# Summing and storing the last 1,024 numbers of a gated attention and FFN step in 16 rows of 64 columns and not in 4 rows of 256

## The chip, the cores and the metric

The kernel runs on one core of a Trainium2 chip. The metric is the device time of one execution in microseconds (us), the median of several runs. The kernel is written by hand for the five engines of a core: TensorE (PE, matmul; PEld is its weight load), VectorE (DVE), ScalarE (ACT), GpSimd (POOL) and SyncE (SP). SP only issues DMAs here. Each engine has an instruction stream of its own, and they meet through semaphores.

## The reference

One token x of 1,024 numbers goes through two branches, and a gate mixes them:

```python
g = sigmoid((x * gate_w).sum())
a = attention(x)      # 32 query heads, 4 key/value heads, cache of 65,536 positions, head size 128, then @ wo
r = sigmoid(x @ w_r)
b = x + r * ((silu(x @ w_gate) * (x @ w_up)) @ w_down)   # F = 3,584
out = g * a + (1 - g) * b                                # 1,024 numbers
```

Everything is float32. Keys, values and weights together are 346 MB and are read once; the output is 4 KB.

## The kernel before, in words

**The stream.** All large inputs are laid out on the host in the order of their use, in tiles of 128 partitions. SP loads the tiles one after the other into three buffers (`stream`, shown as `st`). First come 4 groups of attention, one for each key/value head (L126), then six tiles of 14,336 columns (L128, L132): gate, up and down weights of the FFN. The last two tiles are loaded in pieces, each with a semaphore of its own (`ENDS`, L132), so that PE can begin before the whole tile is there. The last tile holds blocks 14 to 27 of the down weights, and its pieces end behind 6, 10, 12, 13, 13.75 and 14 blocks of 1,024 columns: 3,072, 2,048, 1,024, 512, 384 and 128 KB.

**The attention groups** (the hardware loop from L305) leave the result of the output projection in the PSUM tile `att`. DVE takes it over to `att_sb` in SBUF with gate and residual (L265).

**The FFN.** L382 sums gate and up. ACT and DVE work out the hidden values, and `hp` holds them transposed: 28 blocks of 32 columns, where only the first column of each block is not zero. The down product takes block b of `hp` as the 32 columns of weights and 1,024 columns of the stream as the moving operand. A matmul of 128 x 32 fills one quarter of the array (PSUM partitions 32j to 32j+31), and four of them, j = 0 to 3, run side by side. In the trace a float32 matmul of the program is two MATMULs with a LDWEIGHTS each, so that the counts of the profile are twice those of the code. Blocks 0 to 23 (`EARLY`) are summed into `att` (L392) in 512 columns; DVE adds them to `att_sb` (L277).

**The last four blocks**, 24 to 27, are the part that the change touches (L397 to L414). Here the output is cut in four quarters of 256 columns, and quarter j stands in row 32j. Each quarter is cut again in two pieces, `PIECES`: columns 0 to 191 are summed in the PSUM tile `y`, columns 192 to 255 in the PSUM tile `acc`. At block 26 `att_sb` is added with the selector `halves` as weights (L404), matmul by matmul between those of the stream (L409). For block 27 the host has put the stream's columns in the order of the pieces, so that `y` is complete after the piece of 384 KB and `acc` after the piece of 128 KB. PE runs all this in program order, and `tail()` puts the wait for a piece of the stream ahead of the first matmul that reads it.

**The end.** After the last matmul on `y` (mark "first") ACT copies 128 x 192 from `y` to `fin` in SBUF (L182); after the last matmul on `acc` (mark "last") DVE copies 128 x 64 to the other columns of `fin` (L280). SP waits for ACT (L134) and for DVE (L135), stores rows 0, 32, 64 and 96 of `fin` (L136), waits until the store has landed (L140), clears the semaphores, and the kernel is over.

```python
sp.wait_ge(sems["acted"], ACTED["first"])
sp.wait_ge(sems["d2s"], 1)
sp.dma_start(
    out.rearrange("(j n) -> j n", j=4), fin[::32, :]
).then_inc(sems["done"], 16)
```

At the start of the kernel POOL fills some tiles with zeros, `halves` among them (L147), and DVE writes the selector into column 0 of each of its two halves (L224).

Of the kernel before, what the change touches and what calls it, by code (L numbers as in the profile page):

```python
# [4 lines left out]
AF = mybir.ActivationFunctionType  # L5
# [3 lines left out]
P = 128  # L9
D = 1024  # L10
G = 4
# [3 lines left out]
F = 3584  # L15
CH = 8192
NCH = SK // CH
NM = CH // 512
NB = CH // P
KB = D // P  # L20
NQ = D // 4
FB = F // P
FN = F // 8
SCALE = DH ** -0.5
# [6 lines left out]
TAIL = 14336  # L31
NTAIL = 3 * KB * F // TAIL

ENDS = {NTAIL - 2: [8 * D, TAIL], NTAIL - 1: [6 * D, 10 * D, 12 * D, 13 * D, 13 * D + 768, TAIL]}

PIECES = [(0, 192), (192, NQ)]

EARLY = 24


HEAD = ["q", "qt"] + [f"s{c}" for c in range(NCH)] + ["mx"] + [f"v{c}" for c in range(NCH)] + ["o", "w"]
MARKS = ["dot"] + [f"{m} {g}" for g in range(G) for m in HEAD]
MARKS += ["gate 0", "gate 1", "up 0", "up 1", "early", "first", "last"]
MARK = {m: i + 1 for i, m in enumerate(MARKS)}

LAST = ["s0", "s2", "s4", "s6", "v0", "v2", "v4", "v6", "w"]

ACTS = ["sig"] + [f"{m}{c} {g}" for g in range(G) for m in "se" for c in range(NCH)] + ["hid", "first"]
ACTED = {m: i + 1 for i, m in enumerate(ACTS)}


def gated_mix_kernel(nc, x, vecs, heads, ffn, out):

# [18 lines left out]
    pe, act, dve, pool, sp = nc.tensor, nc.scalar, nc.vector, nc.gpsimd, nc.sync  # L74

    stream = [nc.alloc_sbuf_tensor(f"st{b}", [P, 2 * CH], F32, align_bytes=256)[:, :] for b in range(BUFS)]
    scores = nc.alloc_sbuf_tensor("s", [P, NCH, 512], F32)[:, :, :]
    pts = nc.alloc_sbuf_tensor("pt", [P, 2, 512], F32)[:, :, :]

    hid = scores[:, 0:2, :].rearrange("p a n -> p (a n)")[:, : FB * 32]  # L80
    hp = scores[:, 2:4, :].rearrange("p a n -> p (a n)")[:, : FB * 32]
    att_sb = scores[:, 4, :]
    zeros = scores[:, 5, :]
    fin = scores[:, 7, :NQ]

    o_sb = scores[:, 0, :].rearrange("p (s d) -> p s d", s=4)
    q_sb, lb = scores[:, 1, :], scores[:, 2, :P]
# [1 line left out]
    def sb(name, *shape):  # L89
        t = nc.alloc_sbuf_tensor(name, [P, *shape], F32)  # L90
        return t[tuple(slice(None) for _ in range(len(shape) + 1))]

    xk = sb("xk", 3, KB)
    x_row, ident, ones, md = sb("x_row", 2 * NQ), sb("ident", P), sb("ones", P), sb("md", P)
    sel, sel8, nsel, sel4 = sb("sel", 32), sb("sel8", HG), sb("nsel", HG), sb("sel4", 4)
    half, halves = sb("half", 2), sb("halves", 2, 32)
    xp, qp, op = sb("xp", KB, 32), sb("qp", 4 * (32 + HG)), sb("op", HG, 32)
    dots, dsum, sig, rest = sb("dots", 2, KB), sb("dsum", 2), sb("sig", 2), sb("rest", 2)
    mx, sums, mh, rl = sb("mx", NCH), sb("sums", NCH), sb("mh", HG), sb("rl", HG)
    m1, nb, l1 = sb("m1", 1), sb("nb", 1), sb("l1", 1)  # L100
    gate = sig[:, 0:1]

    def psum(name, *shape):
        return nc.alloc_psum_tensor(name, [P, *shape])[tuple(slice(None) for _ in range(len(shape) + 1))]

    ps_u, ps_f = psum("ps_u", 2, 512), psum("ps_f", 2, 512)
    ps_s = [ps_u[:, i, :] for i in range(2)]
    acc, ps_m, att, y = psum("acc", 512), psum("ps_m", P), psum("att", 512), psum("y", NQ)

    banks = [y, acc]  # L110

    names = ["done", "fed", "x0", "x1", "x2", "acted", "pooled", "marked", "d2p", "d2a", "d2s", "self"]
    names += [f"ld{b}" for b in range(BUFS)] + [f"end{i}" for i in range(sum(map(len, ENDS.values())))]
    sems = {n: nc.alloc_semaphore(n) for n in names}
# [5 lines left out]
    for i in range(G * PER + NTAIL):  # L120
        b = i % BUFS
        if i >= BUFS:
            g, l = divmod(i - BUFS, PER)
            sp.wait_ge(sems["marked"], MARK[f"{LAST[l]} {g}" if g < G else ["gate 0", "gate 1", "up 0"][l]])
        if i < G * PER:
            sp.dma_start(stream[b], heads[i]).then_inc(sems[f"ld{b}"], 16)  # L126
        elif i - G * PER not in ENDS:
            sp.dma_start(stream[b][:, :TAIL], ffn[i - G * PER]).then_inc(sems[f"ld{b}"], 16)  # L128
        else:
            cuts = ENDS[i - G * PER]  # L130
            for c0, c1 in zip([0] + cuts, cuts):
                sp.dma_start(stream[b][:, c0:c1], ffn[i - G * PER, :, c0:c1]).then_inc(sems[f"end{len(ends)}"], 16)  # L132
                ends.append((i, c0, c1))
    sp.wait_ge(sems["acted"], ACTED["first"])  # L134
    sp.wait_ge(sems["d2s"], 1)  # L135
    sp.dma_start(  # L136
        out.rearrange("(j n) -> j n", j=4), fin[::32, :]
    ).then_inc(sems["done"], 16)
    sp.wait_ge(sems["done"], 16)
    sp.sem_clear(range(nums[0], nums[-1] + 1))  # L140

# [4 lines left out]
    for t in (xp, qp, zeros, halves, op):  # L146
# [4 lines left out]
        out=ident, in_=ident, compare_op=ALU.not_equal, fill=1.0, base=0, pattern=[[-1, P]], channel_multiplier=1  # L151
# [3 lines left out]
    acted = []  # L155

    def tell(ins, name):
        acted.append(name)
        return ins.then_inc(sems["acted"])
# [17 lines left out]
            )  # L177
    act.wait_ge(sems["marked"], MARK["gate 1"])
    tell(act.activation(hid.rearrange("p (e n) -> p e n", e=2), ps_f[:, :, :FN], AF.Exp, scale=-1.0), "hid")  # L179
    act.wait_ge(sems["marked"], MARK["first"])  # L180
    c0, c1 = PIECES[0]
    tell(act.activation(fin[:, c0:c1], banks[0][:, : c1 - c0], AF.Copy), "first")  # L182
    assert acted == ACTS


# [35 lines left out]
    then(dve.tensor_copy(sel4, ident.rearrange("p (j h) -> p j h", h=32)[:, :, 0]))  # L221

    then(dve.tensor_add(half, sel4[:, :2], sel4[:, 2:]))
    dve.tensor_copy(halves[:, :, 0], half)  # L224
    then(dve.tensor_reduce(sel8, ident.rearrange("p (a h) -> p h a", h=HG), AX.X, ALU.add))
    then(dve.tensor_scalar_mul(nsel, sel8, -SCALE))
    for g in range(G):
# [10 lines left out]
        for c in range(NCH):  # L238
            acted_on(f"s{c} {g}")
            ins = dve.tensor_reduce(mx[:, c : c + 1], scores[:, c, :], AX.X, ALU.max)  # L240
# [35 lines left out]
    after("early")  # L276
    to_pe(dve.tensor_add(att_sb, att, att_sb))  # L277
    after("last")
    c0, c1 = PIECES[1]
    dve.tensor_copy(fin[:, c0:c1], banks[1][:, : c1 - c0]).then_inc(sems["d2s"])  # L280


    marks = []
# [1 line left out]
    def mark(ins, name):  # L285
        marks.append(name)
        ins.then_inc(sems["marked"])
# [17 lines left out]
    with pe.Fori(0, G):  # L305
        loaded(0)
        for k in range(KB):
            for f in range(2):
                j = 2 * (k % 2) + f
                ins = pe.matmul(  # L310
                    ps_s[0][32 * j : 32 * j + 32, :], xp[:, k, :],
                    unit(0)[:, k * D + f * 512 : k * D + (f + 1) * 512], start=(k < 2), stop=(k >= KB - 2),
                )
        mark(ins, "q")
        take("d2p")
        for e in range(4):
            ins = pe.matmul(ps_m[:, 2 * e : 2 * e + 2], q_sb[:, e * DH : (e + 1) * DH], half, start=True, stop=True)
        mark(ins, "qt")
        take("d2p")
        for c in range(NCH):  # L320
# [3 lines left out]
            for s in range(4):  # L324
                for j in range(4):
                    ins = pe.matmul(  # L326
                        ps_s[c % 2][32 * j : 32 * j + 32, :], qp[:, 32 * s : 32 * s + 32],
                        unit(1 + c)[:, (4 * s + j) * 512 : (4 * s + j + 1) * 512], start=(s == 0), stop=(s == 3),
                    )
# [3 lines left out]
        for c in range(NCH):  # L333
            loaded(1 + NCH + c)
            take("d2p")
            for m in range(NM):
                j = m % 4
                ins = pe.matmul(  # L338
                    acc[32 * j : 32 * j + 32, :], pts[:, c % 2, 32 * m : 32 * m + 32],
                    unit(1 + NCH + c)[:, m * 512 : (m + 1) * 512], start=(c == 0 and m < 4),  # L340
                    stop=(c == NCH - 1 and m >= NM - 4),
                )
# [3 lines left out]
        for s in range(4):  # L346
            ins = pe.matmul(
                ps_m[:, HG : 2 * HG], o_sb[:, s, :], sel[:, HG * s : HG * s + HG], start=(s == 0), stop=(s == 3)
            )
        mark(ins, "o")  # L350
        take("d2p")
        for h in range(HG):
            for f in range(2):
                j = 2 * (h % 2) + f
                ins = pe.matmul(  # L355
                    att[32 * j : 32 * j + 32, :], op[:, h, :],
                    unit(UNITS - 1)[:, h * D + f * 512 : h * D + (f + 1) * 512], start=False, stop=False,
                    skip_group_check=True,
                )
# [4 lines left out]
    def tail(first, n):  # L364
        i, c = divmod(first, TAIL)
        assert c + n <= TAIL
        if i < min(ENDS):
            if c == 0:
                take(f"ld{(G * PER + i) % BUFS}", 16)
        else:  # L370
            for e, (i1, c0, _) in enumerate(ends):
                if (i1 - G * PER, c0) == (i, c):
                    pe.wait_ge(sems[f"end{e}"], 16)
        return stream[(G * PER + i) % BUFS][:, c : c + n]


    for i, part in enumerate(("gate", "up")):
        ps = (ps_f, ps_u)[i]
        for k in range(KB):
            for e in range(2):  # L380
                for j in range(4):
                    ins = pe.matmul(  # L382
                        ps[32 * j : 32 * j + 32, e, :FN], xp[:, k, :], tail((i * KB + k) * F + (2 * j + e) * FN, FN),
                        start=(k == 0), stop=(k == KB - 1),
                    )
# [3 lines left out]
    for b in range(EARLY):  # L389
        for f in range(2):  # L390
            j = 2 * (b % 2) + f
            ins = pe.matmul(  # L392
                att[32 * j : 32 * j + 32, :], hp[:, 32 * b : 32 * b + 32], tail(2 * KB * F + b * D + f * 512, 512),
                start=(b < 2), stop=(b >= EARLY - 2),
            )
    mark(ins, "early")
    for b in range(EARLY, FB):  # L397
        if b == EARLY + 2:
            take("d2p")
        for bank, (c0, c1) in zip(banks, PIECES):  # L400
            n = c1 - c0
            for j in range(4):
                if b == EARLY + 2:
                    pe.matmul(  # L404
                        bank[32 * j : 32 * j + 32, :n], halves[:, j // 2, :],
                        att_sb[:, j % 2 * NQ + c0 : j % 2 * NQ + c1], start=False, stop=False,
                    )
                at = 4 * c0 + j * n if b == FB - 1 else j * NQ + c0
                ins = pe.matmul(  # L409
                    bank[32 * j : 32 * j + 32, :n], hp[:, 32 * b : 32 * b + 32], tail(2 * KB * F + b * D + at, n),  # L410
                    start=(b == EARLY), stop=(b == FB - 1),
                )
            if b == FB - 1:
                mark(ins, "first" if c0 == 0 else "last")  # L414
    assert marks == MARKS


# [29 lines left out]
```

## Time and profile before

| what | value |
|---|---|
| time, median of 3 runs | 805.84 us (805.73 to 806.34) |
| the profiled execution's own time | 805.78 us |
| its span, first to last instruction | 804.5 us |
| read from HBM | 346.05 MB, 430 GB/s over the span |
| PE, PEld, DVE, ACT busy | 51%, 15%, 9%, 6% of the span |
| mean granted TensorE clock | 0.750 |

The profile is of one execution. Its time is 1.3 us more than its span, for what lies around the instructions. The page gives busy shares, the span in 40 slices, the DMA queues, the chain of work that ended last, and the costliest groups of instructions. Views of the trace give single stretches: the timeline has start, duration, engine, line, operation, output<-input, shape and count, and in brackets the idle time before it and what ended it. Matmuls overlap, so a row of eight matmuls lasts from the first start to the last end. The trace's times are counted from the first instruction.

### The profile page before, as it was taken

The page shows a single profiled execution, that of the slowest core. Times are in us where ns is not written, and L with a number is a line of the kernel's source. Part 1 is how long each engine was busy: PE and PEld are TensorE (multiplying, and loading weights), DVE is VectorE, ACT ScalarE, POOL GpSimd, SP SyncE. Part 2 cuts the span into 40 slices and gives each one's busy share as a digit, 9 for nine tenths or more (in the row PEclk, how much of TensorE's full clock was granted, in tenths as well). Part 3 has the DMA queues.
Part 4 walks back from the last instruction along what each step waited for, and adds up shares of the span by engine and source line. Part 5 has one row for each costly group of instructions (what it writes and reads, how often), then busy time and mean ns, then how long its engine had stood idle before and what let it go on. Part 6 is the DMA issues. An engine that isn't in the chain of part 4 may idle for free. (4 is left out here: it accounts for less than half of the span.)

```text
span 804.5 us, 6124 instructions
## 1 busy us (share of the span) xinstructions
PE 407.5 (51%) x2826; PEld 122.0 (15%) x2826; DVE 72.3 (9%) x135; ACT 44.8 (6%) x100; POOL 2.5 (0%) x13
## 2 busy tenths in 40 slices
PE   0544464455654564545544454456444545464466
PEld 0211111111111121111111111112111111121122
DVE  0200010000000020000100110000000100000310
ACT  0000030000000030000000110000000300000000
POOL 1000000000000000000000000000000000000000
PEclk9977767768767677677877586777776866787778
DMA  9999999999999999999999999999999999999998
GB/s 418 417 418 466 415 424 460 417 428 453 420 430 450 424 431 446 427 430 446 427 430 443 430 430 443 430 431 430 440 433 427 443 430 430 429 448 426 439 413 342
DMA packets 7078, 346.20 MB, mean 430 GB/s; under 512 B 918, under 2 KB 1050, under 8 KB 1308
## 3 DMA queue, kind: packets, MB, share of 16 engines
q1 hardware_dynamic: 6920, 346.04, 99.4%
q8 instruction: 8, 0.13, 0.1%
q10 hardware_dynamic: 148, 0.02, 0.0%
q14 instruction: 2, 0.02, 0.0%
HBM read 346.05 MB, written 0.00 MB: 430 GB/s over the span
## 5 line engine op out<-in xcount | busy, mean ns | idle before, releaser
L326 PE MATMUL ps_u<-st,qp 128*32 128x512 f32 x1024 | 152.5, 759 | 149.1 <-PEq L290 149.1
L338 PE MATMUL acc<-st,pt 128*32 128x512 f32 x1024 | 152.3, 757 | 144.1 <-PEq L290 144.1
L338 PEld LDWEIGHTS acc<-st,pt 128*32 128x32 f32 x1024 | 43.5, 135 | 250.0 <-issue 250.0
L326 PEld LDWEIGHTS ps_u<-st,qp 128*32 128x32 f32 x1024 | 41.4, 135 | 256.3 <-issue 256.3
L171 ACT ACTIVATE s<-ps_u 128x512 f32<-128x512 f32 x32 | 19.1, 597 | 560.4 <-PE ps_u L326 560.4
L240 DVE TENSOR_REDUCE mx<-s 128x1 f32<-128x512 f32 x32 | 22.0, 686 | 284.2 <-ACT s L171 284.2
L255 DVE STREAM_TRANSPOSE pt<-s 128x512 f32<-128x512 f32 x32 | 22.7, 711 | 198.0 <-PE acc L338 194.4
L310 PE MATMUL ps_u<-st,xp 128*32 128x512 f32 x128 | 23.3, 893 | 22.1 <-PEq L290 22.1
L382 PE MATMUL ps_u<-st,xp 128*32 128x448 f32 x128 | 17.1, 703 | 16.9 <-PEq L290 16.9
L382 PE MATMUL ps_f<-st,xp 128*32 128x448 f32 x128 | 16.8, 691 | 13.3 <-PEq L290 13.3
L176 ACT ACTIVATE s<-s,nb 128x512 f32<-128x512 f32 x32 | 22.6, 708 | 10.4 <-DVE nb L250 10.4
L392 PE MATMUL att<-st,s 128*32 128x512 f32 x96 | 14.9, 776 | 7.5 <-DMA st<-in_ffn 4.9
L355 PE MATMUL att<-st,op 128*32 128x512 f32 x128 | 14.6, 594 | 2.4 <-PEq L290 2.4
L301 PE MATMUL ps_m<-dsum,ones 128*128 128x2 f32 x2 | 0.6, 350 | 23.5 <-PEq L290 23.5
L310 PEld LDWEIGHTS ps_u<-st,xp 128*32 128x32 f32 x128 | 5.9, 158 | 40.1 <-issue 40.1
L382 PEld LDWEIGHTS ps_u<-st,xp 128*32 128x32 f32 x128 | 5.3, 139 | 28.6 <-issue 28.6
L259 DVE COPY s<-acc 128x512 f32<-128x512 f32 x4 | 2.8, 692 | 71.6 <-PE acc L338 71.6
L382 PEld LDWEIGHTS ps_f<-st,xp 128*32 128x32 f32 x128 | 5.2, 135 | 25.1 <-issue 25.1
L229 DVE COPY s<-ps_u 128x512 f32<-128x512 f32 x4 | 2.8, 692 | 53.5 <-PE ps_u L310 53.5
L179 ACT ACTIVATE s<-ps_f 128x896 f32<-128x896 f32 x1 | 0.9, 917 | 105.4 <-PE ps_f L382 105.4
L392 PEld LDWEIGHTS att<-st,s 128*32 128x32 f32 x96 | 3.7, 134 | 18.6 <-issue 10.7
L332 PE MATMUL ps_m<-md,ones 128*128 128x128 f32 x8 | 1.8, 311 | 8.2 <-PEq L290 8.2
(69 smaller groups left out, 68.9 us busy)
## 6 DMA issues: line engine op xcount, KB each, us to landing
st<-in_ffn SPq DMA_DIRECT2D x4, 7168.0 KB, 43.3
st<-in_ffn SPq DMA_DIRECT2D x2, 3072.0 KB, 37.1
st<-in_ffn SPq DMA_DIRECT2D x1, 4096.0 KB, 34.9
st<-in_ffn SPq DMA_DIRECT2D x1, 2048.0 KB, 36.9
st<-in_ffn SPq DMA_DIRECT2D x1, 1024.0 KB, 38.9
st<-in_heads SPq DMA_DIRECT2D x36, 48.1
st<-in_ffn SPq DMA_DIRECT2D x1, 512.0 KB, 39.7
st<-in_ffn SPq DMA_DIRECT2D x1, 384.0 KB, 40.2
```

Source lines behind the costliest of these rows:

```text
L171: tell(act.activation(scores[:, c, :], ps_s[c % 2], AF.Copy), f"s{c} {g}")
L176: act.activation(t, t, AF.Exp, bias=nb, scale=SCALE, accum_out=sums[:, c : c + 1]), f"e{c} {g}"
L229: to_pe(dve.tensor_copy(q_sb, ps_s[0]))
L240: ins = dve.tensor_reduce(mx[:, c : c + 1], scores[:, c, :], AX.X, ALU.max)
L255: to_pe(dve.transpose(pts[:, c % 2, :], scores[:, c, :]))
L259: to_pe(dve.tensor_copy(o_sb, acc.rearrange("p (s d) -> p s d", s=4)))
L310: ins = pe.matmul(ps_s[0][32 * j : 32 * j + 32, :], xp[:, k, :], unit(0)[:, k * D + f * 512 : k * D + (f + 1) * 512], start=(k < 2), stop= ...
L326: ins = pe.matmul(ps_s[c % 2][32 * j : 32 * j + 32, :], qp[:, 32 * s : 32 * s + 32], unit(1 + c)[:, (4 * s + j) * 512 : (4 * s + j + 1) * ...
L338: ins = pe.matmul(acc[32 * j : 32 * j + 32, :], pts[:, c % 2, 32 * m : 32 * m + 32], unit(1 + NCH + c)[:, m * 512 : (m + 1) * 512], start= ...
L355: ins = pe.matmul(att[32 * j : 32 * j + 32, :], op[:, h, :], unit(UNITS - 1)[:, h * D + f * 512 : h * D + (f + 1) * 512], start=False, sto ...
L382: ins = pe.matmul(ps[32 * j : 32 * j + 32, e, :FN], xp[:, k, :], tail((i * KB + k) * F + (2 * j + e) * FN, FN), start=(k == 0), stop=(k == ...
L392: ins = pe.matmul(att[32 * j : 32 * j + 32, :], hp[:, 32 * b : 32 * b + 32], tail(2 * KB * F + b * D + f * 512, 512), start=(b < 2), stop= ...
```

## The change

The output is cut in 16 rows of 64 columns (`NR`): piece c of quarter j stands in row 32j + 8c. For this the weights are read 8c columns further left (`hp[:, 32b - 8c : ...]`), so that the one column that is not zero stands at column 8c; the columns ahead of it are zeros of the block before. The selector `halves` is 64 columns wide, with its ones in column 32, and is shifted in the same way. All is summed in `y`, which is now 128 x 64; `acc` isn't used here any more, and the mark "first" and ACT's copy are gone. `att_sb` is added ahead of all matmuls of block 26 and not between them. DVE copies `y` in one instruction. SP waits once, and stores 16 rows of 256 bytes (partitions 0, 8, 16, ..., 120). The pieces of the stream are of the same sizes; within block 27 the host orders the columns by c, so that the piece of 384 KB has c = 0 to 2 and the piece of 128 KB has c = 3.

```diff
+NR = NQ // 4
-ENDS = {NTAIL - 2: [8 * D, TAIL], NTAIL - 1: [6 * D, 10 * D, 12 * D, 13 * D, 13 * D + 768, TAIL]}
-PIECES = [(0, 192), (192, NQ)]
+ENDS = {NTAIL - 2: [8 * D, TAIL], NTAIL - 1: [6 * D, 10 * D, 12 * D, 13 * D, 13 * D + 12 * NR, TAIL]}
...
-    fin = scores[:, 7, :NQ]
+    fin = scores[:, 7, :NR]
...
-    half, halves = sb("half", 2), sb("halves", 2, 32)
+    half, halves = sb("half", 2), sb("halves", 2, 64)
...
-    acc, ps_m, att, y = psum("acc", 512), psum("ps_m", P), psum("att", 512), psum("y", NQ)
-    banks = [y, acc]
+    acc, ps_m, att, y = psum("acc", 512), psum("ps_m", P), psum("att", 512), psum("y", NR)
...
-    sp.wait_ge(sems["acted"], ACTED["first"])
     sp.wait_ge(sems["d2s"], 1)
-    sp.dma_start(
-        out.rearrange("(j n) -> j n", j=4), fin[::32, :]
-    ).then_inc(sems["done"], 16)
+    sp.dma_start(out.rearrange("(i n) -> i n", i=16), fin[::8, :]).then_inc(sems["done"], 16)
...
-    act.wait_ge(sems["marked"], MARK["first"])
-    c0, c1 = PIECES[0]
-    tell(act.activation(fin[:, c0:c1], banks[0][:, : c1 - c0], AF.Copy), "first")
...
-    dve.tensor_copy(halves[:, :, 0], half)
+    dve.tensor_copy(halves[:, :, 32], half)
...
     after("last")
-    c0, c1 = PIECES[1]
-    dve.tensor_copy(fin[:, c0:c1], banks[1][:, : c1 - c0]).then_inc(sems["d2s"])
+    dve.tensor_copy(fin, y).then_inc(sems["d2s"])
...
     for b in range(EARLY, FB):
         if b == EARLY + 2:
             take("d2p")
-        for bank, (c0, c1) in zip(banks, PIECES):
-            n = c1 - c0
+            for c in range(4):
+                for j in range(4):
+                    pe.matmul(
+                        y[32 * j : 32 * j + 32, :], halves[:, j // 2, 32 - 8 * c : 64 - 8 * c],
+                        att_sb[:, j % 2 * NQ + c * NR : j % 2 * NQ + (c + 1) * NR], start=False, stop=False,
+                    )
+        for c in range(4):
             for j in range(4):
-                if b == EARLY + 2:
-                    pe.matmul(
-                        bank[32 * j : 32 * j + 32, :n], halves[:, j // 2, :],
-                        att_sb[:, j % 2 * NQ + c0 : j % 2 * NQ + c1], start=False, stop=False,
-                    )
-                at = 4 * c0 + j * n if b == FB - 1 else j * NQ + c0
+                at = 4 * c + j if b == FB - 1 else 4 * j + c
                 ins = pe.matmul(
-                    bank[32 * j : 32 * j + 32, :n], hp[:, 32 * b : 32 * b + 32], tail(2 * KB * F + b * D + at, n),
-                    start=(b == EARLY), stop=(b == FB - 1),
+                    y[32 * j : 32 * j + 32, :], hp[:, 32 * b - 8 * c : 32 * b - 8 * c + 32],
+                    tail(2 * KB * F + b * D + at * NR, NR), start=(b == EARLY and c == 0),
+                    stop=(b == FB - 1 and c == 3),
                 )
-            if b == FB - 1:
-                mark(ins, "first" if c0 == 0 else "last")
+    mark(ins, "last")
...
-    last = down[:, -1].reshape(P, 4, NQ)
-    down[:, -1] = np.concatenate([last[:, :, c0:c1].reshape(P, -1) for c0, c1 in PIECES], axis=1)
+    down[:, -1] = down[:, -1].reshape(P, 4, 4, NR).transpose(0, 2, 1, 3).reshape(P, D)
```

More of the change, by code (lines that the diff above doesn't have):

```diff
@@ L42 @@
 MARKS = ["dot"] + [f"{m} {g}" for g in range(G) for m in HEAD]
-MARKS += ["gate 0", "gate 1", "up 0", "up 1", "early", "first", "last"]
+MARKS += ["gate 0", "gate 1", "up 0", "up 1", "early", "last"]
 MARK = {m: i + 1 for i, m in enumerate(MARKS)}
 LAST = ["s0", "s2", "s4", "s6", "v0", "v2", "v4", "v6", "w"]
-ACTS = ["sig"] + [f"{m}{c} {g}" for g in range(G) for m in "se" for c in range(NCH)] + ["hid", "first"]
+ACTS = ["sig"] + [f"{m}{c} {g}" for g in range(G) for m in "se" for c in range(NCH)] + ["hid"]
 ACTED = {m: i + 1 for i, m in enumerate(ACTS)}
```

## The prediction

> **What bounds the kernel now.** I began with the page's DMA queues and its chain of work that ended last.
>
> ```profile
> q1 hardware_dynamic: 6920, 346.04, 99.4%
> HBM read 346.05 MB, written 0.00 MB: 430 GB/s over the span
> DMA 5%; PE 1%; SPq 0%; DVE 0%; issue 0%
> ```
>
> The 16 DMA engines are busy with the stream for 99.4% of the span, so nearly all of the 804.5 us is the reading of 346 MB, which the change leaves as it is: same bytes, same sizes of pieces. What can move is what lies behind the stream. The chain in order of time shows how it ends:
>
> ```profile
> 759.67 0.33 SPq L132
> 760.00 0.04 issue
> 760.04 0.43 SPq L132
> ...
> 760.52 38.89 DMA st<-in_ffn
> ...
> 799.46 0.53 PE y L409 x8
> ...
> 802.20 0.16 PE acc L409 x8
> 802.36 0.02 issue
> 802.38 0.23 DVE s L280
> ```
>
> From 799.46 on it is PE, then DVE's copy, and behind them stands the store, which this view doesn't reach. So I read the timeline of the last 5 us (start, duration, engine, line, what):
>
> ```profile
> 799.01 0.69 DVE L277 TENSOR_TENSOR s<-att,s 128x512 f32<-128x512 f32 x1 [20.00 <-PE att L392]
> 799.45 0.16 PEld L409 LDWEIGHTS y<-st,s 128*32 128x32 f32 x8 [1.42 <-DMA st<-in_ffn]
> 799.46 0.53 PE L409 MATMUL y<-st,s 128*32 128x192 f32 x8 [0.51 <-DMA st<-in_ffn]
> 799.92 0.51 PE L409 MATMUL y<-st,s 128*32 128x192 f32 x8
> 800.24 0.29 PE L409 MATMUL acc<-st,s 128*32 128x64 f32 x8
> 800.35 0.49 PE L404 MATMUL y<-s,halves 128*32 128x192 f32 x2
> 800.72 0.11 PEld L409 LDWEIGHTS y<-st,s 128*32 128x32 f32 x1 [0.26 <-DMA st<-in_ffn]
> 801.67 0.53 PE L409 MATMUL y<-st,s 128*32 128x192 f32 x8
> 801.96 0.19 PEld L409 LDWEIGHTS acc<-st,s 128*32 128x32 f32 x8
> 802.02 0.29 PE L409 MATMUL acc<-st,s 128*32 128x64 f32 x8
> 802.27 0.33 ACT L182 ACTIVATE s<-y 128x192 f32<-128x192 f32 x1 [58.66 <-PE y L409]
> 802.38 0.23 DVE L280 COPY s<-acc 128x64 f32<-128x64 f32 x1 [2.68 <-PE acc L409]
> 802.70 0.63 SPq L136 DMA_DIRECT2D out<-s  x1
> ```
>
> The reader is to see four stretches. Blocks 24 and 25 run from 799.46 to 800.35. Block 26 with the sum of `att_sb` waits at 800.72 for its piece of the stream, and then PE has work up to 801.67. Block 27 ends with eight matmuls that start from 802.02. Behind them come the copies, 802.27 to 802.61, the store's issue, 802.70 to 803.33, and its landing:
>
> ```profile
> SPq L135 <- DVE s L280: 40.2, 1, 40.2
> SPq L140 <- DMA out<-s: 1.1, 1, 1.1
> ```
>
> SP's last wait but one is for DVE; then it waits 1.1 us for the store, up to about 804.4. Of the 2.4 us behind PE's last starts, 1.7 us are the store.
>
> **The change part by part.**
>
> *PE, the four blocks.* Price 0. A group of eight starts (four j, two passes) lasts 800.35 - 800.24 = 0.11 us at 64 columns and 800.24 - 799.92 = 0.32 us at 192. Three groups of 64 take 0.33 us, so four make a block of 0.44 us in place of 0.43. There are 160 starts in the five rounds (four blocks and `att_sb`) instead of 80, each with a weight load. By these groups it is the columns that cost, not the starts: blocks 24 and 25 end at 800.35 as now.
>
> *The sum of `att_sb` moved ahead of block 26.* Its input is ready at 799.70 (the row of L277), long before. Now two starts of it fit ahead of the wait that ends at 800.72 and the rest come behind; then all 32 can run from 800.35 to 800.79, and block 26 to 801.23. That is 0.4 us earlier than today, and it is worth nothing, since what is late next is the stream: the windows give, per stretch, the length, the busy times, the granted clock, and the DMA engines' share and GB/s.
>
> ```profile
> 792.00:796.00 4.00, 3.83 (x20) 1.00 (x24) 0.00 (x0) 0.00 (x0) 0.00 (x0) 0.50 1.02 436
> 799.40:800.35 0.95, 0.89 (x32) 0.77 (x33) 0.30 (x1) 0.00 (x0) 0.00 (x0) 1.00 0.86 336
> 800.35:801.67 1.32, 1.32 (x44) 0.98 (x36) 0.00 (x0) 0.00 (x0) 0.00 (x0) 1.00 0.46 171
> 801.67:802.38 0.71, 0.65 (x25) 0.35 (x17) 0.00 (x0) 0.11 (x1) 0.00 (x0) 1.00 0.00 0
> ```
>
> Data still come in during the third stretch. The pieces of 512 and 384 KB follow each other: at 430 GB/s the second is 0.9 us behind the first, whose wait ended at 800.72, so it is there at about 801.6, and block 27 can't start much before 801.67. The last 128 KB come 0.3 us later, which fits the weight loads that start at 801.96 (0.29 us behind the block's start, where blocks without a wait have 0.2). In block 27 the three first groups then run from 801.67 to 802.00, and the last eight starts come at 802.00 to 802.02, where they are now. Bounds: 0.05 us earlier to, if the last piece costs a new start, 0.1 later.
>
> *The copies.* Price 0. ACT's copy ends at 802.60 and DVE's at 802.61, so taking ACT's off frees nothing; DVE copies the same 128 x 64 in 0.23 us, from another PSUM tile. Bounds: 0 and 0.02 us.
>
> *SP's waits.* One wait and not two. Between DVE's end (802.61) and the issue (802.70) lie 0.09 us; in the chain an issue with one wait starts about 0.02 us behind what it waited for (759.67). Gain between 0 and 0.07; I take 0.04.
>
> *The store's issue.* The lines of the issues, with minimum, median and maximum in ns:
>
> ```profile
> L126 SPq DMA_DIRECT2D st<-in_heads x36: 327/328/432, 0.7 to 651.4; - x36
> L136 SPq DMA_DIRECT2D out<-s x1: 633/633/633, 802.7 to 802.7; - x1
> L163 ACTq DMA_DIRECT2D x_row<-in_x x1: 1058/1058/1058, 1.3 to 1.3; - x1
> ```
>
> Loads of 128 rows are issued in 0.33 us, the store of 4 rows takes 0.63, the load of 2 rows 1.06. Fewer rows take longer, not more. Sixteen rows lie between 0.33 and 0.63, a gain of 0.30 to 0. I take the whole 0.30, on the inference that what costs is the number of engines left out: 16 rows can be shared out among the 16 DMA engines as 128 can, 2 and 4 can't.
>
> *The store's landing.* Price 0. After the issue 1.1 us pass. Sixteen packets of 256 bytes take the place of four of 1 KB. The DMA view of 802.70 to 804.50 in 40 slices of 0.045 us shows the packets themselves:
>
> ```profile
> GB/s 0 0 0 0 0 0 0 0 0 0 0 0 0 0 0 0 0 0 0 0 0 0 0 0 0 0 0 23 46 23 0 0 0 0 0 0 0 0 0 0
> ```
>
> They move in three slices, 0.135 us from 803.92 on; 0.6 us pass before and 0.35 behind them. Smaller packets can save no more than 0.1. The other way, 16 packets to finish instead of 4 could at most double the time behind them: 0.35 later. The nearest row is this store itself, with the same 4 KB, so I take its 1.1 us unchanged. [...]
>
> *At the start.* Price 0. POOL fills a `halves` of twice the size, and DVE writes its ones into another column.
>
> ```profile
> 2.23 0.15 POOL L147 MEMSET halves<- 128x64 f32 x1
> 22.88 0.17 DVE L205 COPY xp<-xk 128x8 f32<-128x8 f32 x1 [22.88 <-DMA xk<-in_vecs]
> ```
>
> Even 0.15 us more on POOL at 2.2 us is covered by DVE's first instruction, which waits for a load until 22.88; without that cover it would be 0.15.
>
> *Sum.* 0 + 0 + 0 - 0.04 - 0.30 + 0 = -0.34 us, all of it behind PE. The profiled execution took 805.78 (span 804.5 and 1.3 around it): 805.44. The median of the runs is 0.06 above it: 805.5. With the small bounds together (0.05 + 0.02 + 0.07 + 0.30 + 0.1 gained; 0.1 + 0.35 lost) the case spans 805.3 to 806.3; its own range is 805.2 to 805.8.
>
> **The rivals.**
>
> *A, PE can't start 64-column matmuls that fast (slower).* The groups of 64 columns stand between wide ones, during which the next instructions can queue up; 160 narrow starts in a row are nowhere in this trace. What it holds over a long stretch is 32 starts in 0.89 us, 28 ns each. At that pace 160 starts take 4.48 us from 799.46, to 803.94 instead of 802.13: 1.81 later, less the 0.34 gained, 807.3. It makes the kernel slower from 19 ns a start on: (802.13 - 799.46 + 0.34) / 160. Against it stand the two groups of eight in 0.11 us, 14 ns a start. [...]
>
> *B, the store is no cheaper (no gain).* The issue stays at 0.63, which gives 805.8, or the small writes land 0.35 later, which gives 805.85, or both, 806.2. For it: no row with 16 rows, no small write. Against it: the three issue rows.
>
> *C, PE waits for its own instructions.* The code grows by 160 PE instructions.
>
> ```profile
> q8 instruction: 8, 0.13, 0.1%
> ```
>
> Eight fetches of 16 KB took 0.1% of 16 engines' span, between 0.05 and 0.15%, so 0.8 to 2.4 us each. One more of them in the open gives 806.3 to 807.9. Against it: block 27 has no idle time but that for the stream, so instructions are there in advance.
>
> **How the numbers follow.** Forecast 0.65 at 805.5; B 0.17 (805.8 to 806.2); A 0.10 (806.3 to 807.6); C 0.05; 0.03 for anything else, the clock below among it. The three runs lie 0.6 us apart, which I add below: low 805.0. Above, the range takes in B and A's 807.3, leaving out less than 2 in 10 in all. 0.2% is 1.6 us, about what a measurement of this kernel can tell from no change: faster means below 804.2, which no term here reaches (0.03); slower means above 807.45, the upper parts of A and C and what I don't see (0.09); within, 0.88.
>
> **What would show it.** Right: in the changed kernel L136 takes about 0.33 us and the wait of L140 about 1.1; the groups of eight on `y` follow every 0.11 us; block 27 starts at the landing of its piece, and DVE's copy about 0.7 us behind that. Wrong: groups further apart than 0.15 us (A); L136 at 0.6 or L140's wait at 1.4 (B); an idle stretch of PE in blocks 24 to 27 with no DMA behind it (C). The prediction also fails if the stream itself gets faster or slower, or if the last stage runs at the granted clock of 0.50 that the stretch at 792 shows and not at 1.00; then each of the five rounds takes 0.44 us more, in either kernel.

## The result, and the profile after

The changed kernel takes 807.21 us, median of 22 runs (806.72 to 807.71), against 805.84 (805.63 to 806.34) for the kernel before: a ratio of 1.0016, 95% interval 1.0010 to 1.0022. It is 1.4 us slower: 0.16%, and the slowest run of the kernel before (806.34) is still faster than the fastest of the changed one (806.72). The profiled execution took 807.03 us, with a span of 805.7, against 805.78 and 804.5.

The chain of work that ended last, in the changed kernel, in order of time (start, duration, what), its last seven pieces:

```profile
760.95 40.79 DMA st<-in_ffn
801.75 0.04 issue
801.79 0.42 PE y L401 x14
802.22 0.92 issue
803.14 0.51 PE y L401 x18
803.65 0.02 issue
803.67 0.23 DVE s L272
```

In the middle of block 27 stands a piece of 0.92 us called "issue": PE waits for nothing that the profile shows. The timeline of the changed kernel has the same stretch by instruction:

```profile
799.60 0.94 PEld L401 LDWEIGHTS y<-st,s 128*32 128x32 f32 x64 [1.42 <-DMA st<-in_ffn]
799.60 1.10 PE L401 MATMUL y<-st,s 128*32 128x64 f32 x64 [0.51 <-DMA st<-in_ffn]
800.52 0.63 PE L394 MATMUL y<-s,halves 128*32 128x64 f32 x32
800.97 0.63 PE L401 MATMUL y<-st,s 128*32 128x64 f32 x32
801.79 0.42 PE L401 MATMUL y<-st,s 128*32 128x64 f32 x14 [0.20 <-DMA st<-in_ffn]
803.14 0.49 PE L401 MATMUL y<-st,s 128*32 128x64 f32 x18 [0.92 <-issue]
803.14 0.33 PEld L401 LDWEIGHTS y<-st,s 128*32 128x32 f32 x17 [1.09 <-issue]
803.67 0.23 DVE L272 COPY s<-y 128x64 f32<-128x64 f32 x1 [3.82 <-PE y L401]
803.92 0.55 SPq L134 DMA_DIRECT2D out<-s  x1
```

Blocks 24 and 25 with their 64 starts run from 799.60 to the first start of `att_sb` at 800.52, which is 0.11 us for a group of eight. The narrow matmuls run at the pace of the prediction. Block 27 starts 14 of its 32 matmuls and then stops for over a microsecond, on PE and PEld alike: 1.14 us lie between the last start before the gap, at 802.00, and the next one. Then the last 18 matmuls and 17 weight loads follow. The windows of the stretches (length, PE, PEld, DVE, ACT and POOL busy, granted clock, DMA share, GB/s) say what it isn't:

```profile
801.79:802.10 0.31, 0.31 (x14) 0.26 (x15) 0.00 (x0) 0.00 (x0) 0.00 (x0) 1.00 0.00 0
802.10:803.14 1.04, 0.12 (x9) 0.00 (x0) 0.00 (x0) 0.00 (x0) 0.00 (x0) 1.00 0.00 0
803.14:803.67 0.53, 0.49 (x18) 0.33 (x17) 0.00 (x0) 0.00 (x0) 0.00 (x0) 1.00 0.00 0
```

The clock is at 1.00 throughout, no other engine works, and in the gap the DMA engines move nothing. The last piece of the stream isn't the cause either: it is read by the last eight matmuls, and the stop comes ten matmuls ahead of them.

The account of the 1.25 us between the two profiled executions, from their timelines: block 27 starts 0.12 later (801.79 against 801.67), with the stream of that execution; from there DVE's copy starts after 1.88 us (803.67) instead of 0.71 (802.38), which is 1.17 more; and from DVE's start to the end of the span it is 2.05 instead of 2.09, 0.04 less. The gap is nearly all of the loss, and far more than what the end gains.

### The profile page after: what moved, and what is told of

Its sections match the earlier page's. It is cut to its first block, busy times and chain, and to the rows that moved or that the text cites. A ratio compares the mean times of both kernels' runs of the same rounds, so it can differ in the third digit from the quotient of the medians.

```text
span 805.7 us, 6282 instructions
## 1 busy us (share of the span) xinstructions
PE 399.5 (50%) x2906; PEld 120.0 (15%) x2906; DVE 72.4 (9%) x135; ACT 44.5 (6%) x99; POOL 2.6 (0%) x13
## 5 line engine op out<-in xcount | busy, mean ns | idle before, releaser
L318 PE MATMUL ps_u<-st,qp 128*32 128x512 f32 x1024 | 150.8, 751 | 152.6 <-PEq L282 152.6
L330 PE MATMUL acc<-st,pt 128*32 128x512 f32 x1024 | 146.8, 734 | 152.5 <-PEq L282 152.5
L330 PEld LDWEIGHTS acc<-st,pt 128*32 128x32 f32 x1024 | 41.4, 132 | 254.8 <-issue 254.8
L302 PE MATMUL ps_u<-st,xp 128*32 128x512 f32 x128 | 20.3, 791 | 14.1 <-PEq L282 14.1
L347 PE MATMUL att<-st,op 128*32 128x512 f32 x128 | 19.4, 760 | 2.4 <-PEq L282 2.4
L347 PEld LDWEIGHTS att<-st,op 128*32 128x32 f32 x128 | 5.1, 134 | 13.4 <-issue 13.4
```

Of the source, the lines that this page charges most:

```text
L302: ins = pe.matmul(ps_s[0][32 * j : 32 * j + 32, :], xp[:, k, :], unit(0)[:, k * D + f * 512 : k * D + (f + 1) * 512], start=(k < 2), stop= ...
L318: ins = pe.matmul(ps_s[c % 2][32 * j : 32 * j + 32, :], qp[:, 32 * s : 32 * s + 32], unit(1 + c)[:, (4 * s + j) * 512 : (4 * s + j + 1) * ...
L330: ins = pe.matmul(acc[32 * j : 32 * j + 32, :], pts[:, c % 2, 32 * m : 32 * m + 32], unit(1 + NCH + c)[:, m * 512 : (m + 1) * 512], start= ...
L347: ins = pe.matmul(att[32 * j : 32 * j + 32, :], op[:, h, :], unit(UNITS - 1)[:, h * D + f * 512 : h * D + (f + 1) * 512], start=False, sto ...
```

## The experiments

"Record" means an instruction of PE as the trace lists them (matmuls, weight loads, and some 130 semaphore and loop instructions), counted from the start of the program; one in the loop counts once for each pass. The changed kernel has 5,942 of them, 160 more than the kernel before, and 35 of them lie behind the gap.

The theory at first was this. PE comes to the end of the instructions that have been fetched, and waits for the next ones. The trace has a packet (one transfer of a DMA engine) of 16 KB on the queue for instructions (q8) that starts at 800.59, 1.4 us before PE stops. The DMA view of 800 to 801 us shows it: one packet of 0.02 MB, for 8.0% of what 16 engines have in 1 us, which is 1.28 us.

```profile
q8 instruction: 1, 0.02, 8.0%
```

The rivals: N, sixteen narrow rows in one PSUM tile stop PE by themselves; S, the store of 16 rows costs the time.

### Fewer instructions in the last blocks

```diff
-EARLY = 24
+EARLY = 25
```

> Block 24 is summed in 512 columns into att like the blocks before it (EARLY 25), so PE has 4 matmuls of the program there and not 16; with two passes and a weight load for each that is 48 instructions fewer than in the changed kernel, and att_sb is added ahead of block 27. Theory (PE comes to the end of the instructions that are fetched; 35 records were left behind the gap): the gap in block 27 is gone, 805.6 to 806.1 us. Rival N (sixteen narrow rows in one PSUM tile, or block 27 itself, stop PE): blocks 26 and 27 are as in the changed kernel, the gap stays, about 807.2. Rival S (the store of 16 rows costs the time): about 807.2.

Measured: 805.95 us against 805.96 before on the same chip, ratio 1.0000 (0.9991 to 1.0009). The gap is gone. (A block of `att` is 2 matmuls in the code and not 4, so the kernel has 56 instructions fewer and not 48.) Blocks 25 to 27, their 16 rows and the store are as in the changed kernel, which speaks against N and S.

### As many instructions more in the kernel before

```diff
     for i, part in enumerate(("gate", "up")):
+    # ahead of this loop, in the kernel before:
+    for _ in range(40):
+        pe.matmul(ps_m[:32, :2], xp[:, 0, :], dsum, start=True, stop=True)
```

> The kernel before, its last blocks, copies and store untouched, with 40 matmuls of 2 columns into an unused part of ps_m ahead of the gate, where PE waits for the stream: 160 PE instructions more, as many as the change adds. Theory: PE meets the same gap of about 1.1 us with some 35 records left, now within the wide matmuls of block 27 or 26, and the time is 806.8 to 807.3 us. Rivals N and S: no gap, 805.8.

Measured: 805.96 against 805.96, ratio 1.0000 (0.9991 to 1.0010), and no gap. The theory missed: this kernel has 5,942 records like the changed one, and PE doesn't stop. The number of instructions is not enough.

### The changed kernel with less code ahead of the end

```diff
                 for j in range(4):
+                    if i == 0 and k in (1, 2) and (k - 1) * 8 + e * 4 + j < 12:   # 6 in the second run
+                        continue
                     ins = pe.matmul(
                         ps[32 * j : 32 * j + 32, e, :FN], xp[:, k, :], tail(...)
```

> The changed kernel, leaving out 12 of the gate's matmuls (part of the gate's sum is not computed), 48 PE instructions fewer some 50 us ahead of the end; the end's code is that of the changed kernel. Theory: 48 is more than the 35 left behind the gap, so no gap, 805.6 to 806.1 us. Rivals N and S: 807.2.

> As the run without 12 matmuls of the gate, but only 6 left out: 24 PE instructions fewer. Theory: the gap stays, with about 11 records behind it and not 35; 806.8 to 807.3 us. If the gap came from the load on the DMA or from time and not from a count of instructions, it would not move by 24 records. Rivals N and S: 807.2 too, with 35 records behind the gap.

Measured: 805.93 us with 48 fewer (1.0000, 0.9991 to 1.0009), without a gap; 806.82 with 24 fewer (1.0010, 1.0000 to 1.0019), with one. Timeline of the run with 24 fewer, where L403 is the line of the stream's matmuls:

```profile
801.63 0.63 PE L403 MATMUL y<-st,s 128*32 128x64 f32 x26 [0.17 <-DMA st<-in_ffn]
803.26 0.31 PE L403 MATMUL y<-st,s 128*32 128x64 f32 x6 [0.99 <-issue]
803.26 0.15 PEld L403 LDWEIGHTS y<-st,s 128*32 128x32 f32 x5 [1.16 <-issue]
```

Behind the gap are 6 matmuls and 5 weight loads, 11 records; the kernel has 5,918. 5,942 - 35 and 5,918 - 11 are both 5,907. PE stops at the same record, wherever in block 27 that falls, so N falls: it is a border in the instruction stream. The two kernels without a gap so far that have the changed end, with 5,886 records (block 24 in wide matmuls) and 5,894 (48 fewer), end before it. It was now clear what the run with 40 small matmuls in the kernel before had shown: it too crosses record 5,907, and it doesn't stop there.

So theory F (F for fetch): the instructions come in blocks, and the next block is asked for some 250 records ahead of the border. (An estimate from the changed kernel's packets of 16 KB on q8: those at 740.84 and 774.69 us start 250 records apart. The next one, at 800.59, starts some 360 behind.) It needs some 3.3 us to be usable, and the changed kernel alone runs through these records faster than that: its record 5,651, which is 256 ahead of the border, starts at 799.80, it is at the border at 802.00, 2.2 us later, and goes on at 803.14, after 3.3. The rival was T, that it is the number of instructions up to the end.

### More instructions in the changed kernel

The same small matmuls as above, ahead of the gate, in the changed kernel: 8, 4 and 40 of them.

```diff
+    for _ in range(8):   # 4, 40 in the other runs
+        pe.matmul(ps_m[:32, :2], xp[:, 0, :], dsum, start=True, stop=True)
     for i, part in enumerate(("gate", "up")):
```

> The changed kernel, nothing left out, with 8 matmuls of 2 columns ahead of the gate, where PE waits for the stream: 32 PE instructions more. Theory F (PE's instructions come in blocks of 256; the next block is asked for when PE enters the last one it has, and is there about 3.3 us later; the gap comes because the 256 instructions from the request to the border now take only some 2.2 us): the border moves 32 records nearer to the start of block 24, so 67 records are left behind it, the request falls ahead of the wait for block 24 and about 1.2 us earlier, and the gap shrinks to 0 to 0.2 us: 805.8 to 806.2. Rival T (it is the number of instructions up to the end that is over a limit): the gap stays or grows, 807.0 or more.

> As the run with 8 matmuls more, but with 4 (16 PE instructions). Theory F: the request still falls behind the wait for block 24, about 0.1 us after its start; the border is met 51 records before the end, and the gap stays, 0.9 to 1.3 us: 806.7 to 807.3. Rival T: the same time.

> The changed kernel with the 40 matmuls ahead of the gate (160 PE instructions) which left the kernel before as fast as it was. Theory F: the border lies 195 records before the end, in blocks 24 to 26, and its request in the wide matmuls of the blocks before, where PE waits for the stream for microseconds: no gap, 805.8 to 806.1, with more instructions than any kernel here. Rival T: a gap, 807.2 or more.

Measured: with 32 instructions more 806.91 (1.0013, 1.0004 to 1.0022), with 16 more 806.84 (1.0012, 1.0003 to 1.0021), with 160 more 805.90 against 805.88 (1.0000, 0.9991 to 1.0009). The last one decides: the kernel with the most instructions of all has no gap and is as fast as the kernel before. T falls. For 16 the expectation of the time held, that of the stop did not: 0.67 us from start to start in the profiled execution (806.65 us) and not 0.9 to 1.3. For 32 it was wrong in both, with a stop of 1.31 us: I had put the request two records ahead of the wait for block 24, which ended at 799.42 there, and the packet started behind it, at 800.08.

Timeline with 32 more, then with 16 more:

```profile
800.79 0.62 PE L403 MATMUL y<-st,s 128*32 128x64 f32 x30
802.50 0.72 PE L403 MATMUL y<-st,s 128*32 128x64 f32 x34 [1.09 <-issue]
802.50 0.55 PEld L403 LDWEIGHTS y<-st,s 128*32 128x32 f32 x33 [1.25 <-issue]
```

```profile
800.76 1.12 PE L403 MATMUL y<-st,s 128*32 128x64 f32 x38
802.33 0.61 PE L403 MATMUL y<-st,s 128*32 128x64 f32 x26 [0.45 <-issue]
802.33 0.44 PEld L403 LDWEIGHTS y<-st,s 128*32 128x32 f32 x25 [0.61 <-issue]
```

Behind the gap stand 34 + 33 = 67 records of 5,974, and 26 + 25 = 51 of 5,958. That is record 5,907 in both again. And with 160 more, where the border lies 195 records ahead of the end:

```profile
799.64 1.10 PE L403 MATMUL y<-st,s 128*32 128x64 f32 x64 [0.50 <-DMA st<-in_ffn]
800.55 0.63 PE L396 MATMUL y<-s,halves 128*32 128x64 f32 x32
801.00 0.63 PE L403 MATMUL y<-st,s 128*32 128x64 f32 x32
801.80 0.65 PE L403 MATMUL y<-st,s 128*32 128x64 f32 x32 [0.17 <-DMA st<-in_ffn]
802.52 0.22 DVE L272 COPY s<-y 128x64 f32<-128x64 f32 x1 [2.62 <-PE y L403]
```

From the start of block 27 to DVE's copy it is 0.72 us, as in the kernel before (0.71).

### A little more: 48 instructions

The same edit with 12 small matmuls.

> The changed kernel with 12 matmuls of 2 columns ahead of the gate: 48 PE instructions more, where 32 left a gap of 1.31 us and 160 none. With 32 the request came just behind the wait for block 24 and not ahead of it, as I had expected, so it lies a few records later than 256 ahead of the border at record 5907. Theory F, so mended: with 48 the request falls some 10 to 15 records ahead of that wait, so about 1 us earlier; the next block is there 2.4 to 2.6 us behind the fetch's record, at 801.5 to 801.7, just when block 27 may start. A gap stands in block 26, 83 records before the end, but it lies beside the wait for the stream: 805.8 to 806.1. Rival T (the number of instructions): 806.8 or more, as with 32. Rival D (it is the load on the DMA queue that makes the fetch late): 806.8 too, since the stream is the same.

Measured: 806.08 against 805.87, ratio 1.0001 (0.9992 to 1.0010). Sixteen instructions more than the run with 32, and 0.8 us less. The time was as F expected. The way was not: there is no gap at all, not even one beside the wait for the stream. Timeline of block 27 and the copy:

```profile
802.00 0.65 PE L403 MATMUL y<-st,s 128*32 128x64 f32 x32 [0.20 <-DMA st<-in_ffn]
802.72 0.23 DVE L272 COPY s<-y 128x64 f32<-128x64 f32 x1 [2.74 <-PE y L403]
```

The trace's packets on the queue for instructions and PE's stop, in us from the start of the span, side by side. The third column counts the records that PE has started when the packet starts:

| kernel | the 16 KB packet starts | records by then | PE's last start before the gap | goes on | from packet to going on |
|---|---|---|---|---|---|
| changed | 800.59 | 5,768 | 802.00 | 803.14 | 2.55 |
| 24 fewer | 800.68 | 5,775 | 802.05 | 803.26 | 2.58 |
| 16 more | 799.95 | 5,725 | 801.66 | 802.33 | 2.38 |
| 32 more | 800.08 | 5,751 | 801.19 | 802.50 | 2.42 |
| 48 more | 796.06 | 5,633 | no gap | | |
| 160 more | 783.20 | 5,639 | no gap | | |
| before, 160 more | 784.29 | 5,649 | no gap | | |

In all four kernels with a gap PE goes on 2.4 to 2.6 us behind the start of that packet. Where the packet started 5.4 us or more before PE came to the border (801.45 with 48 more), there is none. The three kernels that cross the border without a stop have one packet more, which starts 0.3 to 1.0 us after PE has crossed it (with 48 more at 802.22). The packet itself lasts 0.9 to 1.3 us; what the rest of the 2.5 us is, the trace doesn't show. With 48 more the packet starts in the middle of the stream, so a busy stream doesn't keep it back as such, and rival D falls as the sole cause.

What isn't settled is what sets the start of the packet. In the kernels without a stop it starts 258 to 274 records ahead of the border, in those with one 132 to 182. Between 32 and 48 more instructions it jumps by 4 us, and a request at one fixed record, ahead of a wait for the stream in the one kernel and behind it in the other, doesn't explain that: with 32 more PE has the same 5,633 records behind it at 797.29, and the packet starts 2.8 us later. It may have stood in line behind the stream's packets there; that was not measured, and the question stays open.

### The price of the store's issue

Two more kernels change the shape of the store alone, the first on top of the one with 32 more instructions, the second of the one with 160 more.

```diff
-    sp.dma_start(out.rearrange("(i n) -> i n", i=16), fin[::8, :]).then_inc(sems["done"], 16)
+    sp.dma_start(out.rearrange("(i n) -> i n", i=128), fin[:, :8]).then_inc(sems["done"], 16)
```

```diff
+    sp.dma_start(out.rearrange("(i n) -> i n", i=64), fin[::2, :16]).then_inc(sems["done"], 16)
```

> The changed kernel with the 8 small matmuls, storing 128 rows of 32 bytes and not 16 of 256, so that what is stored isn't the result. The price of the store's issue by its rows: by the inference of the prediction (it is the number of DMA engines left out that costs) 128 rows are issued in as long as 16 rows, 0.55 us in the changed kernel; if it goes by rows alone, in another time, 0.33 us as the loads of 128 rows or over 0.6.

> The changed kernel with the 40 small matmuls, storing 64 rows of 64 bytes, so that what is stored isn't the result. Four rows were issued in 0.63 us, 16 in 0.55, 128 in 0.35. If the price falls with the rows, 0.4 to 0.5 us; if only the 128 rows of a full tile are cheap, 0.55.

The issue's line (minimum, median, maximum in ns) in the changed kernel, with 128 rows and with 64 rows:

```profile
L134 SPq DMA_DIRECT2D out<-s x1: 552/552/552, 803.9 to 803.9; - x1
```

```profile
L134 SPq DMA_DIRECT2D out<-s x1: 348/348/348, 803.5 to 803.5; - x1
```

```profile
L134 SPq DMA_DIRECT2D out<-s x1: 541/541/541, 802.9 to 802.9; - x1
```

Four rows are issued in 0.63 us, 16 in 0.55, 64 in 0.54, 128 in 0.35. That isn't the number of DMA engines left out, by which 16 and 64 rows would have cost as little as 128; nor does it fall evenly with the rows. The packets of the stores say the same: 8, 32, 80 and 144 of them, which is one for each row and besides these 4, 16, 16 and 16 of 4 bytes. By that count 16, 64 and 128 rows are alike, and their prices are not. Only the 128 rows of a full tile come near the loads' 0.33. (One run of each was made, of 807.57 and 806.05 us; they are looked at for the store alone.) SP's last wait, from the end of the issue to the landing, in the changed kernel:

```profile
SPq L136 <- DMA out<-s: 1.2, 1, 1.2
```

It was 1.1 with four rows of 1 KB. So sixteen writes of 256 bytes land about 0.1 us later, and of the 0.08 us that the issue gains little is left.

## Why the prediction was wrong

The forecast was 0.34 us less, the profiled executions differ by 1.25 us more. Of the 1.59 us between the two, 1.17 are the gap, a cost that the sum had at nothing (rival C below). 0.30 are missing at the end, which gained 0.04 and not 0.34, mostly by the store's issue. The last 0.12 are the later start of block 27 in that execution.

**The bound and PE's price.** Right. The end of the stream sets when block 27 starts, the groups of eight last 0.11 us, and `att_sb` ahead of block 26 ends in the shade of the stream: PE waits 0.2 us for the piece of block 27. Without the gap, the time from block 27's start to DVE's copy is 0.72 us, as I had it. Rival A, a floor for narrow starts, doesn't show at this size: 128 starts in a row keep 14 ns each (799.60 to 801.38), and the 28 ns of the prediction came from a stretch in which half of the starts were 192 columns wide.

**The copies and SP's waits.** Right in size. DVE's copy is 0.23 us again, and the issue starts 0.02 us behind its end instead of 0.09.

**The store's issue.** Wrong, and the only term of the sum with any weight: 0.30 us expected, 0.08 measured. The sum took the upper end of its own bounds (0.30 to 0) on an inference, that the price falls with the engines left out, and 0.54 us for 64 rows refutes it.

**The store's landing.** Nearly right: 1.2 for 1.1, well below the upper bound of 0.35 more.

**Rival C.** This is what happened, and I gave it 0.05. Its price of 0.8 to 2.4 us held the 1.17 that the gap costs. The step of the prediction that failed is the sentence against it, that block 27 has no idle time but that for the stream, "so instructions are there in advance". That is true of the kernel before and says nothing about twice as many instructions in the same time: from block 24 on the kernel before has 161 records, and the border lies 125 behind its end. The changed kernel has 321, and it meets the border 2.4 us after it starts on them. What I should have asked is how long a block of instructions lasts and how long the next one takes to come. The number to begin with stood in the page of the profile (eight packets of 16 KB on q8). In the trace of the kernel before the last three of them start 230 and 329 records apart (742.66, 774.56 and 801.41 us), and in the kernel with 160 more the last three ahead of the border 258 and 256. 256 records of this kernel's narrow kind last about 1.8 us (32 records in 0.22 us of two groups), and 2.4 to 2.6 us were measured from the packet's start until PE went on.

The measured 807.21 lies on the other side of "before" than the forecast of 805.5. That it still lies inside the range is luck: the upper end stood there for the 807.3 of rival A, which didn't happen. A change within 0.2% had the largest chance, and 1.0016 is within it, for another reason than the one given.

A version that beats both kernels was not found. The changed kernel without its gap is as fast as the kernel before (805.90 against 805.88 with 160 instructions more, 805.95 against 805.96 with block 24 in wide matmuls), so the 16 rows themselves are worth nothing that can be measured here.

## What to carry to other kernels

Count instructions, not only columns: cutting the same work into narrower matmuls at an unchanged pace per column can outrun the fetch of the engine's own code, as it did here at the end of a stretch without a loop, where PE met the border 1.41 us after the packet had started and went on 2.55 us after it. An idle stretch that the chain calls "issue" (0.92 us), on PE and PEld together, with the data there, was the mark of it; whether it stays at the same instruction when code is added or left out far ahead of it is the test. For the store of a result as small as 4 KB, the price was that of one issue and one landing: here about 1.7 us together for 4, 16 and 64 rows, and 1.45 for 128 (0.35 and 1.1), with one run each for 64 and 128.

## What the runs showed of the hardware that was not expected

Adding instructions made the changed kernel faster: 48 or 160 more, where PE waits for the stream anyway, bring its 807.21 us down to 806.08 and 805.90, while 16 or 32 leave 806.84 and 806.91. The border stood at record 5,907 in all four kernels that stopped. In the run with 32 more, two of eleven executions took 808.06 and 808.29 us while the others lay between 806.64 and 807.00. The profiled one is the second of them; its span is only 805.3 us, and its trace has one more packet of instructions, at 807.14, behind the last instruction. Its time is 3.0 us more than its span, where the kernel before has 1.3. The run that stores 128 rows shows the same: a packet at 806.85, behind the last instruction, and a time 2.6 us more than its span (807.57 and 805.0). That a fetch past the program's end can delay the end is suggested by the two and was not tried.
